# Six channel products moved into the attention steps, and kept products stored as upper and lower digits on two halves of the partitions

## The chip, the cores and the metric

One core of a Trainium2 chip runs the whole kernel. The time is the device time of one execution in microseconds (us); a profile is of one execution, taken by the hardware profiler, and its span is some 1.8 us shorter than that execution's own time. It can be of the slowest or of the fastest of a kernel's few executions, so spans are compared with care. Engines: PE is TensorE, PEld its weight loads, DVE is VectorE, ACT is ScalarE, POOL is GpSimd, SP is SyncE.

## The reference, cut to what matters

```python
x = attention(q, k, v, s)            # 8 batches x 576 tokens x 512 channels (8 heads x 64)
X = rfft(x, axis=1)                  # 64 modes are kept
Yr = Xr @ w_r - Xi @ w_i             # one 512x512 pair of weights for each mode
Yi = Xr @ w_i + Xi @ w_r
y = irfft(Y, n=576, axis=1)
u = x + y
return u + relu(u @ w_ch)            # w_ch: 512x512
```

The weights `w_r` and `w_i` are read once from memory, in 128 pieces, and most of the kernel's time passes while they arrive. The kernel uses `u @ w_ch = x @ w_ch + irfft(Y @ w_ch)`: the first term (the *product* of a pair of token tiles) needs no weight of the modes and can be made early and *kept*; the second, called v, is made chunk by chunk as the modes come.

## The kernel before

The work is cut into 18 pairs of 128-token tiles. Attention takes 32 steps; the modes of the fourth and last quarter of the channels then come in 8 chunks of 8 modes (0 to 7). Between these chunks the kernel makes the products of 16 pairs and keeps them in one of two ways. With way "e" the value is stored as two fp16 numbers, upper and lower digits, and TensorE puts it back (the *seed*: a product with the identity); with way "s" it is stored in fp32 and ScalarE puts it back.

```python
ways = dict(zip(kept, "esesessesesseses"))
def keep(i):
    x_times_wch(i, True)                      # 8 matmuls into zs[i], 128x1024 of PSUM
    ...
    if ways[i] == "e":                        # upper digits, then what is left
        nc.scalar.copy(out=z1s[i][:, 0], in_=zs[i])
        nc.vector.tensor_tensor(out=z1s[i][:, 1], in0=zs[i], in1=z1s[i][:, 0], op=ALU.subtract)
    else:
        nc.scalar.copy(out=z1s[i], in_=zs[i])
...
def seed(i):                                  # way "e": 4 matmuls of 128x512
    for x in range(2):
        for y in range(2):
            nc.tensor.matmul(zs[i][:, x, :], ident16h, z1s[i][:, y, x, :], start=(y == 0), ...)
...
TAKE = (3, 3, 1, 2, 4, 3)                     # works after chunks 0 to 5
for c in range(NCK - 2):
    yb = modes(NG - 1, c)
    for x in range(TAKE[c] - 1):
        work()                                # transposes one x, and makes the product of the one before
    yt = y_transposed(yb)
    work()
    y_times_wch(c, yt)                        # v of chunk c, then spread by a small DMA
...                                           # chunk 6, start_u(0), add_y of u
yb = modes(NG - 1, NCK - 1)                   # chunk 7: waits for the last weight
...                                           # its y and v
for i in range(NPRE):
    add_y(z_of(i), i, 1, slice(0, GK))        # v of chunks 0 to 6 into the first two pairs
```

`add_y` is the inverse transform of what has been spread. After chunk 7 the *tail* adds everything up for the 18 pairs and stores the result.

The softmax here doesn't subtract the row's maximum and nothing guards it: scores larger than these inputs give would overflow.

Of the kernel before, what the change touches and what calls it, by code (L numbers as in the profile page):

```python
# [9 lines left out]
FP32 = mybir.dt.float32  # L10
# [8 lines left out]
def kernel(  # L19
# [11 lines left out]
    nc = tc.nc  # L31
# [14 lines left out]
    MC = 8  # L46
    NCK = NM // MC
    WM = 4
    WB = 17
    LA = 3  # L50
    NF = NT - 1
    R = S // (P // 2)
# [23 lines left out]
    G_np[:, 1, :S] = -(cmv[:, None] * np.sin(ang.T))  # L76
    G_np = G_np.reshape(P, SP).astype(np.float16)

    d_ident16h = nc.inline_tensor(ident_np.astype(np.float16), name="c_ident16h").ap()
    d_ident32 = nc.inline_tensor(ident_np, name="c_ident32").ap()  # L80
    d_negm = nc.inline_tensor(
        np.concatenate([negm_np, negm4_np], axis=1).astype(np.float32), name="c_negm"
# [13 lines left out]
    y_acc = gp.tile([P, NCK, DM], FP32, name="y_acc")  # L96

    xs = [gp.tile([P, 5, 2, B, NM], BF16, name=f"xs{i}") for i in range(2)]
    ident16h = gp.tile([P, P], FP16, name="ident16h")
    Ff_sb = gp.tile([P, NT, 3 * NM], FP16, name="Ff_sb")  # L100
    G_sb = gp.tile([P, SP], FP16, name="G_sb")
    wch_sb = gp.tile([P, DT, DM], FP16, name="wch_sb")
    wpool = ctx.enter_context(tc.tile_pool(name="w_sb", bufs=WB))
    spool = ctx.enter_context(tc.tile_pool(name="small_sb", bufs=2))
    auxpool = ctx.enter_context(tc.tile_pool(name="aux_psum", bufs=2, space=PSUM))

# [78 lines left out]
    NE = len(early)  # L185
    wt = {}

    def loads_w(upto):
        todo = []
        while len(wt) < min(upto, len(wq)):  # L190
            g, c, ri, par = key = wq[len(wt)]
            if len(wt) < NE:
                t = early[len(wt)]
            else:
                t = wpool.tile([P, WM, DM], BF16, name="w_sb", tag="w")
            src = (moe_w_r, moe_w_i)[ri]
            todo.append((
                t,
                src[c * MC + par : (c + 1) * MC : 2, g * P : (g + 1) * P, :].rearrange("m p e -> p m e"),
            ))  # L200
            wt[key] = t
        return todo
# [14 lines left out]
    W0 = 3  # L217
    on_chip = []
    for n in range(N):
        w = W0 + (WB + NE - W0) * (n + 1) // (B + 1) if n < B else on_chip[-1] + 4  # L220
        on_chip.append(min(w, WB + (NE if used[n] < NE else used[n])))


    nc.sync.dma_start(out=s_sb, in_=s.rearrange("b h t -> (b h) t"))
# [3 lines left out]
    load(first[:2])  # L228
    load(loads_w(W0), first[2:] + tails0 + second)
    nc.sync.dma_start(out=Ff_sb, in_=d_Ff.rearrange("(T p) c -> p T c", p=P))  # L230
    nc.sync.dma_start(out=ident16h, in_=d_ident16h)
    nc.sync.dma_start(out=G_sb, in_=d_G)

    zero = ap_.tile([P, 16], FP32, name="zero")
# [60 lines left out]
    def transposes(n, which):  # L295
        if n >= N:
            return
        src = loaded[n][which]
        dA, dB = ((qtA, qtB), (ktA, ktB))[which]
        g, b = divmod(n, B)  # L300
        ps = trpool.tile([P, R, RP], BF16, name="tr_ps", tag="tr")
        for r in range(R):
            for h in range(2):
                rows = slice(D * h, D * h + D)
                nc.tensor.transpose(ps[rows, r, :], src[rows, r, :], ident16[rows, rows])  # L305
        for dst, rows in ((dA, slice(0, D)), (dB, slice(D, P))):
            copy = (nc.vector.tensor_copy, nc.scalar.copy)[which == 1 and dst is dB]
            copy(  # L308
                out=dst[n % NQ][rows, :].rearrange("d (p r) -> d p r", r=R),
                in_=ps[rows].rearrange("d r p -> d p r"),  # L310
            )
# [131 lines left out]
        nc.sync.dma_start(out=yv[16 * c : 16 * c + 16, :, which, :], in_=rows)  # L443


    with tc.tile_pool(name="sc_psum", bufs=2, space=PSUM) as scpool, \
            tc.tile_pool(name="tr_psum", bufs=1, space=PSUM) as trpool, \
            tc.tile_pool(name="av_psum", bufs=1, space=PSUM) as avpool:
        cum_rows(0)
        transposes(0, 0)  # L450
        transposes(0, 1)
        load(loads_qkv(2))
        pad_p()
        for n in range(N):
            if n in (0, 2):
                nc.vector.memset(xs[n // 2].rearrange("p k r b m -> p (k r b m)").bitcast(FP32), 0.0)
            tails_due = loads_tails(n // B + 1)[n % B - 3 : n % B - 2] if 2 < n % B < 5 else []
            load(loads_qkv(n + LA) + tails_due, loads_w(on_chip[n]))
            cum_rows(n + 1)
            scores(n, 0)  # L460
            av(n - 1, 1)
            transposes(n + 1, 0)
            scores(n, 1)
            transposes(n + 1, 1)
            fft(n - 1)
            av(n, 0)
            for c in mode_steps.get(n, []):
                modes(c // NCK, c % NCK)
            if n == N // 2:
                nc.gpsimd.dma_start(out=wch_sb, in_=moe_w_ch.rearrange("(dt p) e -> p dt e", p=P))  # L470
        av(N - 1, 1)
        fft(N - 1)
    load(loads_w(len(wq)))
    at.close()




    pairs = [((b, T), (b, T + 1)) for b in range(B) for T in range(0, NF, 2)]
    for i, b in ((4, 0), (10, B // 2)):  # L480
        pairs.insert(i, ((b, NF), (b + 2, NF)))
    NPRE = 2
    kept = list(range(NPRE, len(pairs)))


    ways = dict(zip(kept, "esesessesesseses"))

    finpool = ctx.enter_context(tc.tile_pool(name="fin_sb", bufs=1))
    yv = finpool.tile([P, B, 2, DM], FP16, name="yv")
# [11 lines left out]
    places = [finpool.tile([P, 4 * DM], BF16, name=f"z1_{i}") for i in range(NLOC)]  # L501
    places.append(old[:, 4 * DM : 8 * DM])
    places += [y_acc[:, c : c + 2, :].rearrange("p c e -> p (c e)").bitcast(BF16) for c in (0, 2)]
    xts, z1s, zs = {}, {}, {}

    def parts(b, T):

# [24 lines left out]

    def keep(i):
        x_times_wch(i, True)
        j = kept.index(i)
        if j < len(places):
            t = places[j]
        else:
            t = wpool.tile([P, WM, DM], BF16, name="z1", tag="w").rearrange("p m e -> p (m e)")
        if ways[i] == "e":  # L540
            z1s[i] = t.bitcast(FP16).rearrange("p (y x e) -> p y x e", y=2, x=2)
            nc.scalar.copy(out=z1s[i][:, 0], in_=zs[i])
            nc.vector.tensor_tensor(
                out=z1s[i][:, 1], in0=zs[i], in1=z1s[i][:, 0], op=ALU.subtract
            )
        else:
            z1s[i] = t.bitcast(FP32).rearrange("p (x e) -> p x e", x=2)
            nc.scalar.copy(out=z1s[i], in_=zs[i])  # L548

    def y_transposed(yb):  # L550
        ps = auxpool.tile([P, DT, P], FP16, name="yt_ps", tag="aux")
# [29 lines left out]
            i = ahead.pop(0)  # L581
            keep(i)

    order_z = list(kept)
    TAKE = (3, 3, 1, 2, 4, 3)
    us, rs = {}, {}
    GK = P - 2 * MC

# [64 lines left out]
    for c in range(NCK - 2):  # L653
        yb = modes(NG - 1, c)
        for x in range(TAKE[c] - 1):
            work()
        yt = y_transposed(yb)
        work()
        y_times_wch(c, yt)
    work()  # L660
    assert not order_z and not ahead
# [9 lines left out]

    start_u(0)
    add_y(us[0], 0, 0, slice(0, GK))
    yb = modes(NG - 1, NCK - 1)

    yt = spool.tile([P, DT, P], FP16, name="yt_sb", tag="yt")
# [14 lines left out]
        nc.vector.tensor_copy(out=vb[:, cols], in_=vp)  # L691
    spread(NCK - 1, 1, vb)
    for i in range(NPRE):
        add_y(z_of(i), i, 1, slice(0, GK))
    for i in range(NPRE):
        for cols in halves:
            add_last(z_of(i), i, vb, cols)
        relu(i, 2 - i)
# [5 lines left out]
    def seed(i):  # L704
        if ways.get(i) in ("e", "s"):
            zs[i] = zpool.tile([P, 2, DM], FP32, name="z_ps", tag="z")
        if ways.get(i) == "s":
            nc.scalar.copy(out=zs[i], in_=z1s[i])
        elif ways.get(i) == "e":
            for x in range(2):  # L710
                for y in range(2):
                    nc.tensor.matmul(  # L712
                        zs[i][:, x, :], ident16h, z1s[i][:, y, x, :],
                        start=(y == 0), stop=False, skip_group_check=True,
                    )

    def pre(i):
# [51 lines left out]
```

## Time and profile before

| | before |
|---|---|
| median of 4 runs beside the changed kernel | 461.33 us (460.58 to 462.08) |
| span in the profile, mean granted clock | 460.4 us, 0.873 |
| bytes read and written by transfers | 95.16 MB by the queues, 207 GB/s |
| the last weights' modes end | 422.06 us |
| first seed of the tail | 427.39 us |

The times are read from the timeline. Below is TensorE's timeline of before between 405 and 428 us; the columns are start, duration, engine and line, operation, tiles, sizes, the count, and in brackets the idle time before it with what ended it.

```profile
410.80 1.12 PE L419 MATMUL yp<-w_sb,xs 128*32 128x512 bf16 x16
412.72 0.40 PE L553 MATMUL yt_ps<-ident16h,y_sb 128*128 128x128 f16 x4 [0.26 <-DVE y_sb L433]
414.14 1.03 PE L561 MATMUL v_ps<-wch_sb,yt_sb 128*128 128x512 f16 x4
415.00 3.62 PE L528 MATMUL z_ps<-wch_sb,xs 128*128 128x512 f16 x16
421.61 0.45 PE L419 MATMUL yp<-w_sb,xs 128*32 128x512 bf16 x4 [1.29 <-DMA w_sb<-in_moe_w_i_dram]
```

The modes of chunk 6 (410.80) run as soon as the works are done. TensorE then waits 0.26 us for a y, and 1.29 us for the last weight at 421.61.

### The profile page before, as it was taken

How to read it: one execution, taken by the hardware profiler on the slowest of the kernel's cores; microseconds unless marked ns; L12 is line 12 of the kernel's file. 1: busy time of each engine (PE TensorE's matmuls, PEld its weight loads, DVE VectorE, ACT ScalarE, POOL GpSimd, SP SyncE). 2: the span in 40 equal slices, each digit the busy share in tenths (PEclk: the TensorE clock that was granted, in tenths of full speed). 3: DMA queues.
4: the chain of work that ended last, by engine and by line, in shares of the span. 5: the costliest groups of instructions: out<-in, count | busy, mean ns of one | idle time of the engine just before them, and what ended most of it. 6: DMA issues, size and time to landing. Idle time of an engine off the chain costs nothing.

```text
span 460.4 us, 10238 instructions
## 1 busy us (share of the span) xinstructions
PE 342.2 (74%) x4153; PEld 217.0 (47%) x4185; DVE 233.2 (51%) x521; ACT 218.4 (47%) x376; POOL 183.0 (40%) x269
## 2 busy tenths in 40 slices
PE   1779888974667668876666757567959858988995
PEld 1456666653445446654444534344635424544432
DVE  6775666663334346644334443334445625562675
ACT  1585876563444427744244342444602303340895
POOL 6754555544445455434544434444422222100000
PEclk9997999998777879978778795777878979999999
DMA  9999999999999999999999999999999999994697
GB/s 173 200 203 204 201 202 203 203 204 204 204 202 203 203 201 203 204 204 203 203 202 205 205 204 204 204 204 204 204 210 210 212 215 213 211 212 89 229 309 296
DMA packets 110063, 95.16 MB, mean 207 GB/s; under 512 B 28544, under 2 KB 105216, under 8 KB 110016
## 3 DMA queue, kind: packets, MB, share of 16 engines
q0 software_dynamic: 98960, 81.81, 112.2%
q1 hardware_dynamic: 11056, 12.70, 9.1%
q8 instruction: 33, 0.54, 0.4%
q14 instruction: 14, 0.11, 0.1%
HBM read 164.66 MB, written 9.44 MB: 378 GB/s over the span
## 4 chain that ended last, share of the span: by engine, by line
DMA 70%; PE 21%; issue 3%; DVE 3%; POOL 2%; SPq 0%; DVEq 0%; POOLq 0%
DMA w_sb<-in_moe_w_i_dram 31%; DMA w_sb<-in_moe_w_r_dram 25%; DMA q<-in_q_dram 7%; PE sc_ps L346 3%; PE sc_ps L340 2%; DMA wch_sb<-in_moe_w_ch_dram 2%; DMA v<-in_v_dram 2%; PE av_ps L375 2%; PE z_ps L593 2%; PE u_ps L612 2%; PE u_ps L593 2%; PE tr_ps L305 2%; PE yp L419 1%; PE z_ps L712 1%; PE z_ps L528 1%
## 5 line engine op out<-in xcount | busy, mean ns | idle before, releaser
L354 ACT ACTIVATE p_sb<-sc_ps,cumt_sb 128x576 f16<-128x576 f32 (+1 forms) x256 | 142.2, 635 | 57.2 <-PE sc_ps L346 57.0
L208 POOL DMA_DIRECT2D w_sb<-in_moe_w_i_dram x60 | 45.1, 753 | 74.8 <-PE yp L419 19.6
L208 POOL DMA_DIRECT2D w_sb<-in_moe_w_r_dram x60 | 45.2, 754 | 69.7 <-DMA w_sb<-in_moe_w_r_dram 33.2
L208 POOL DMA_DIRECT2D v<-in_v_dram x72 | 50.8, 707 | 36.0 <-DMA v<-in_v_dram 9.3
L305 PE MATMUL tr_ps<-ident,q 64*64 64x64 bf16 x576 | 18.8, 219 | 57.5 <-DMA q<-in_q_dram 57.5
L340 PE MATMUL sc_ps<-negm,ident 128*128 128x256 bf16 x256 | 58.2, 315 | 0.2
L419 PE MATMUL yp<-w_sb,xs 128*32 128x512 bf16 x480 | 37.0, 415 | 19.6 <-DMA w_sb<-in_moe_w_i_dram 18.7
L308 DVE COPY qtA<-tr_ps 64x576 bf16<-64x576 bf16 x32 | 23.8, 743 | 52.7 <-PE tr_ps L305 52.5
L325 ACT ACTIVATE p<-sc_ps,cumt 128x64 f16<-128x64 f32 x32 | 10.1, 314 | 84.1 <-PE sc_ps L321 84.1
L308 DVE COPY ktA<-tr_ps 64x576 bf16<-64x576 bf16 x32 | 24.0, 750 | 44.6 <-PE tr_ps L305 44.6
L375 PE MATMUL av_ps<-v,p_sb 128*128 128x65 f16 x1024 | 45.4, 199 | 0.0
L305 PEld LDWEIGHTS <-q 64*64 64x64 bf16 x576 | 14.8, 130 | 60.4 <-DMA q<-in_q_dram 59.5
L375 PEld LDWEIGHTS <-p_sb 128*128 128x128 f16 x1024 | 40.4, 101 | 5.2 <-issue 1.2
L346 PE MATMUL sc_ps<-qtB,ktB 128*128 128x64 bf16 (+2 forms) x160 | 37.6, 343 | 4.2 <-issue 3.1
L346 PE MATMUL sc_ps<-qtA,ktA 65*128 65x512 bf16 (+2 forms) x192 | 37.7, 306 | 0.5 <-DMA qtA<-ncum_sb 0.5
L528 PE MATMUL z_ps<-wch_sb,xs 128*128 128x512 f16 x144 | 37.0, 405 | 0.7 <-ACT z L548 0.7
L419 PEld LDWEIGHTS <-xs 128*32 128x32 bf16 x512 | 21.7, 172 | 29.6 <-issue 26.1
L380 DVE TENSOR_REDUCE den<-av_ps 128x5 f32<-128x10 f32 x64 | 10.8, 169 | 47.0 <-PE av_ps L375 46.9
L385 DVE TENSOR_TENSOR x_all<-av_ps,rcp 128x320 f16<-128x320 f32 x64 | 31.5, 492 | 2.2
L346 PEld LDWEIGHTS <-ktB 128*128 128x128 bf16 x192 | 23.9, 125 | 17.2 <-issue 8.8
L308 ACT COPY ktB<-tr_ps 64x576 bf16<-64x576 bf16 x32 | 20.3, 634 | 21.6 <-DVE ktA L308 21.1
L305 PE MATMUL tr_ps<-ident,k 64*64 64x64 bf16 x576 | 17.9, 213 | 15.0 <-DVE qtB L308 8.4
(96 smaller groups left out, 498.5 us busy)
## 6 DMA issues: line engine op xcount, KB each, us to landing
w_sb<-in_moe_w_r_dram POOLq DMA_DIRECT2D x60, 512.0 KB, 11.9
w_sb<-in_moe_w_i_dram POOLq DMA_DIRECT2D x60, 512.0 KB, 11.9
q<-in_q_dram POOLq DMA_DIRECT2D x32, 144.0 KB, 9.9
k<-in_k_dram POOLq DMA_DIRECT2D x32, 144.0 KB, 10.3
v<-in_v_dram POOLq DMA_DIRECT2D x72, 64.0 KB, 10.0
out_dram<-r_sb SPq DMA_DIRECT2D x16, 256.0 KB, 2.5
out_dram<-r_w SPq DMA_DIRECT2D x16, 256.0 KB, 2.6
x_all<-in_moe_w_i_dram POOLq DMA_DIRECT2D x3, 512.0 KB, 9.9
```

The costliest lines, as they stand in the source:

```text
L208: nc.gpsimd.dma_start(out=dst, in_=src)
L305: nc.tensor.transpose(ps[rows, r, :], src[rows, r, :], ident16[rows, rows])
L308: copy(out=dst[n % NQ][rows, :].rearrange("d (p r) -> d p r", r=R), in_=ps[rows].rearrange("d r p -> d p r"),)
L340: nc.tensor.matmul(ps[:, bass.ds(w * S, W)], ident16, negm[:, bass.ts(r, W)], start=True, stop=False, skip_group_check=True,)
L346: nc.tensor.matmul(ps[:, c0 : c0 + i1 - i0], keys[:, w, r, :], qt[:, i0:i1], start=False, stop=True, skip_group_check=True,)
L354: nc.scalar.activation(out=pt[:, poff[x] : poff[x] + S - w * W], in_=ps[:, w * S : (w + 1) * S - w * W], func=ACTF.Exp, bias=cumt_sb[:, x, ...
L375: nc.tensor.matmul(ps[:, I, r : r + NCH], lhsT, rhs, start=(i == 0), stop=(i == len(todo) - 1), skip_group_check=True,)
L380: nc.vector.tensor_reduce(out=den, in_=ps[:, :, 0 : VW : NCH], axis=mybir.AxisListType.X, op=ALU.add)
L385: nc.vector.tensor_tensor(out=x_all[:, g, b, :, D * h : D * h + D], in0=ps[:, :, 1 : NCH], in1=rcp.unsqueeze(2).to_broadcast([P, NT, D]), ...
L419: nc.tensor.matmul(ps[32 * cg : 32 * cg + 32, :], cols[:, c0 : c0 + 32, c * MC + 2 * cg + par], wt[(g, c, ri, par)][:, cg, :], start=(x == ...
L528: nc.tensor.matmul(z[:, x, :], xts[i][:, x, dt, :], wch_sb[:, dt, :], start=(dt == 0), stop=(last and dt == DT - 1), skip_group_check=True,)
L593: nc.tensor.matmul(dst[x][r, :], G_sb[rows, bass.ds(T * P, r.stop - r.start)], yv[rows, bb, which, :], start=start, stop=True, skip_group_ ...
```

## The change

The intent is to shorten the tail, the only part that doesn't wait for weights. Seeds of way "e" become cheaper on TensorE: the upper digits lie on one half of the partitions and the lower on the other, so one matmul of 64 columns with a "folding" identity adds them, and two such matmuls run beside each other on two column groups. Six products move into the last six attention steps. To find room for these six before attention's buffers are free, the ring of 17 weight buffers is divided into 11 and 6, and the 6 are given to kept products from weight 76 on. `TAKE` gets fewer works, and the `add_y` of the first two pairs goes ahead of the last modes.

```diff
-    WB = 17
+    WA, WB = 11, 6
...
-    ways = dict(zip(kept, "esesessesesseses"))
+    ways = dict(zip(kept, "eseseseseseseses"))
+    first_pairs = [i for i in kept if pairs[i][0][1] < NF and pairs[i][0][0] <= 3]   # six pairs
...
+        for y in range(2):                   # keep_product, way "e"
+            own, other = (slice((P // 2) * h, (P // 2) * (h + 1)) for h in (y, 1 - y))
+            nc.scalar.copy(out=z1s[i][own, y, xx], in_=z[own])
+            nc.vector.tensor_tensor(
+                out=z1s[i][other, y, xx], in0=z[own], in1=z1s[i][own, y, xx], op=ALU.subtract
+            )
...
+                first_transposed(i, 0)       # in attention step n, between its own work
...
-    TAKE = (3, 3, 1, 2, 4, 3)
+    TAKE = (2, 2, 1, 2, 0, 3)
...
+    for i in range(NPRE):
+        add_y(z_of(i), i, 1, slice(0, GK))
     yb = modes(NG - 1, NCK - 1)
...
-                        zs[i][:, x, :], ident16h, z1s[i][:, y, x, :],
-                        start=(y == 0), stop=False, skip_group_check=True,
+                        zs[i][(P // 2) * y : (P // 2) * (y + 1), x, :], fold16h, z1s[i][:, y, x, :],
+                        start=True, stop=False, skip_group_check=True,
+                        tile_position=(0, (P // 2) * y),
```

More of the change, by code (lines that the diff above doesn't have):

```diff
@@ L77 @@
     G_np = G_np.reshape(P, SP).astype(np.float16)
-    d_ident16h = nc.inline_tensor(ident_np.astype(np.float16), name="c_ident16h").ap()
+    ident16h_np = np.concatenate([ident_np, ident_np[:, : P // 2] + ident_np[:, P // 2 :]], axis=1)
+    d_ident16h = nc.inline_tensor(ident16h_np.astype(np.float16), name="c_ident16h").ap()
     d_ident32 = nc.inline_tensor(ident_np, name="c_ident32").ap()
@@ L98 @@
     xs = [gp.tile([P, 5, 2, B, NM], BF16, name=f"xs{i}") for i in range(2)]
-    ident16h = gp.tile([P, P], FP16, name="ident16h")
+    ident16h2 = gp.tile([P, P + P // 2], FP16, name="ident16h")
+    ident16h, fold16h = ident16h2[:, :P], ident16h2[:, P:]
     Ff_sb = gp.tile([P, NT, 3 * NM], FP16, name="Ff_sb")
@@ L102 @@
     wch_sb = gp.tile([P, DT, DM], FP16, name="wch_sb")
-    wpool = ctx.enter_context(tc.tile_pool(name="w_sb", bufs=WB))
+    wpool = ctx.enter_context(tc.tile_pool(name="w_sb", bufs=WA))
+    wpool2 = ctx.enter_context(tc.tile_pool(name="w2_sb", bufs=WB))
     spool = ctx.enter_context(tc.tile_pool(name="small_sb", bufs=2))
@@ L186, with ring_of @@
     wt = {}
+    LW2 = 76
+    def ring_of(k):
+        if k < NE:
+            return None
+        return int(k < LW2 and (k - NE) % (WA + WB) >= WA)
     def loads_w(upto):
@@ L191, in loads_w @@
             g, c, ri, par = key = wq[len(wt)]
-            if len(wt) < NE:
+            i = ring_of(len(wt))
+            if i is None:
                 t = early[len(wt)]
             else:
-                t = wpool.tile([P, WM, DM], BF16, name="w_sb", tag="w")
+                t = (wpool, wpool2)[i].tile([P, WM, DM], BF16, name="w_sb", tag="w")
             src = (moe_w_r, moe_w_i)[ri]
@@ L219 @@
     for n in range(N):
-        w = W0 + (WB + NE - W0) * (n + 1) // (B + 1) if n < B else on_chip[-1] + 4
-        on_chip.append(min(w, WB + (NE if used[n] < NE else used[n])))
+        w = W0 + (WA + WB + NE - W0) * (n + 1) // (B + 1) if n < B else on_chip[-1] + 5
+        nt, ring = 0, ([], [])
+        while nt < min(w, len(wq)):
+            i = ring_of(nt)
+            if i is not None:
+                depth = (WA, WB)[i]
+                if len(ring[i]) >= depth and ring[i][-depth] >= used[n]:
+                    break
+                ring[i].append(nt)
+            nt += 1
+        on_chip.append(nt)
     nc.sync.dma_start(out=s_sb, in_=s.rearrange("b h t -> (b h) t"))
@@ L230 @@
     nc.sync.dma_start(out=Ff_sb, in_=d_Ff.rearrange("(T p) c -> p T c", p=P))
-    nc.sync.dma_start(out=ident16h, in_=d_ident16h)
+    nc.sync.dma_start(out=ident16h2, in_=d_ident16h)
     nc.sync.dma_start(out=G_sb, in_=d_G)
@@ L443, in spread, with kept_place, keep_product, first_transposed @@
         nc.sync.dma_start(out=yv[16 * c : 16 * c + 16, :, which, :], in_=rows)
+    pairs = [((b, T), (b, T + 1)) for b in range(B) for T in range(0, NF, 2)]
+    for i, b in ((4, 0), (10, B // 2)):
+        pairs.insert(i, ((b, NF), (b + 2, NF)))
+    NPRE = 2
+    kept = list(range(NPRE, len(pairs)))
+    ways = dict(zip(kept, "eseseseseseseses"))
+    first_pairs = [i for i in kept if pairs[i][0][1] < NF and pairs[i][0][0] <= 3]
+    z1s, xts1 = {}, {}
+    def kept_place(i, t):
+        if ways[i] == "e":
+            z1s[i] = t.bitcast(FP16).rearrange("p (y x e) -> p y x e", y=2, x=2)
+        else:
+            z1s[i] = t.bitcast(FP32).rearrange("p (x e) -> p x e", x=2)
+    def keep_product(i, xx, z):
+        if ways[i] != "e":
+            nc.scalar.copy(out=z1s[i][:, xx], in_=z)
+            return
+        for y in range(2):
[4 more added lines that the diff above has]
+            )
+    def first_transposed(i, x):
+        b, T = pairs[i][x]
+        ps = auxpool.tile([P, DT, P], FP32, name="xt_ps", tag="aux")
+        for dt in range(DT):
+            nc.tensor.matmul(
+                ps[:, dt, :], x_all[:, dt, b, T, :], ident16h, start=True, stop=True,
+                skip_group_check=True,
+            )
+        xts1[i, x] = spool.tile([P, DT, P], FP16, name="xt1", tag="yt")
+        nc.vector.tensor_copy(out=xts1[i, x], in_=ps)
+    def first_product(i, x):
+        if x == 0:
+            t = wpool2.tile([P, WM, DM], BF16, name="z1", tag="w").rearrange("p m e -> p (m e)")
+            kept_place(i, t)
+        ps = auxpool.tile([P, DM], FP32, name="z1_ps", tag="aux")
+        for dt in range(DT):
+            nc.tensor.matmul(
+                ps, xts1[i, x][:, dt, :], wch_sb[:, dt, :], start=(dt == 0), stop=(dt == DT - 1)
+            )
+        keep_product(i, x, ps)
     with tc.tile_pool(name="sc_psum", bufs=2, space=PSUM) as scpool, \
@@ L463 @@
             scores(n, 1)
+            i = first_pairs[n - N + len(first_pairs)] if n >= N - len(first_pairs) else None
+            if i is not None:
+                first_transposed(i, 0)
             transposes(n + 1, 1)
@@ L466 @@
             av(n, 0)
+            if i is not None:
+                first_product(i, 0)
+                first_transposed(i, 1)
             for c in mode_steps.get(n, []):
                 modes(c // NCK, c % NCK)
+            if i is not None:
+                first_product(i, 1)
             if n == N // 2:
@@ L474 @@
     at.close()
-    pairs = [((b, T), (b, T + 1)) for b in range(B) for T in range(0, NF, 2)]
-    for i, b in ((4, 0), (10, B // 2)):
-        pairs.insert(i, ((b, NF), (b + 2, NF)))
-    NPRE = 2
-    kept = list(range(NPRE, len(pairs)))
-    ways = dict(zip(kept, "esesessesesseses"))
     finpool = ctx.enter_context(tc.tile_pool(name="fin_sb", bufs=1))
@@ L503 @@
     places += [y_acc[:, c : c + 2, :].rearrange("p c e -> p (c e)").bitcast(BF16) for c in (0, 2)]
-    xts, z1s, zs = {}, {}, {}
+    xts, zs = {}, {}
     def parts(b, T):
@@ L534, in keep @@
         x_times_wch(i, True)
-        j = kept.index(i)
+        j = late.index(i)
         if j < len(places):
@@ L539, in keep @@
             t = wpool.tile([P, WM, DM], BF16, name="z1", tag="w").rearrange("p m e -> p (m e)")
-        if ways[i] == "e":
-            z1s[i] = t.bitcast(FP16).rearrange("p (y x e) -> p y x e", y=2, x=2)
-            nc.scalar.copy(out=z1s[i][:, 0], in_=zs[i])
-            nc.vector.tensor_tensor(
-                out=z1s[i][:, 1], in0=zs[i], in1=z1s[i][:, 0], op=ALU.subtract
-            )
-        else:
-            z1s[i] = t.bitcast(FP32).rearrange("p (x e) -> p x e", x=2)
-            nc.scalar.copy(out=z1s[i], in_=zs[i])
+        kept_place(i, t)
+        keep_product(i, slice(0, 2), zs[i])
     def y_transposed(yb):
@@ L582, in work @@
             keep(i)
-    order_z = list(kept)
-    TAKE = (3, 3, 1, 2, 4, 3)
+    late = [i for i in kept if i not in first_pairs]
+    order_z = list(late)
+    TAKE = (2, 2, 1, 2, 0, 3)
     us, rs = {}, {}
@@ L657 @@
         yt = y_transposed(yb)
-        work()
+        if TAKE[c]:
+            work()
         y_times_wch(c, yt)
@@ L693 @@
     for i in range(NPRE):
-        add_y(z_of(i), i, 1, slice(0, GK))
-    for i in range(NPRE):
         for cols in halves:
```

## The prediction

> **What bounds the kernel now.** I read the page's slices first, then the chain that ended last, then the timeline of the last 60 us, then the waits of the attention steps.
>
> ```profile
> PE   1779888974667668876666757567959858988995
> DMA  9999999999999999999999999999999999994697
> GB/s 173 200 203 204 201 202 203 203 204 204 204 202 203 203 201 203 204 204 203 203 202 205 205 204 204 204 204 204 204 210 210 212 215 213 211 212 89 229 309 296
> ```
>
> A slice is 11.5 us. For 36 slices the DMA row stands at 9 and the rate at 200 to 215 GB/s, while PE is often at 6 or 7: up to about 418 us the weight stream (w_r, w_i) sets the pace. Then PE is at 8 and 9: the last 40 us are TensorE's. The chain says the same:
>
> ```profile
> DMA 70%; PE 21%; issue 3%; DVE 3%; POOL 2%; SPq 0%; DVEq 0%; POOLq 0%
> ```
> ```profile
> 398.48 23.09 DMA w_sb<-in_moe_w_i_dram
> 421.61 0.48 PE yp L419 x3
> ```
>
> The last weight, issued at 398.48, lands at 421.6; the last mode chunk (c = 7) can only then be ended. The tail is 460.4 - 421.6 = 38.8 us. From 427.39 (first seed) to 455.4 TensorE has 16 pairs of 6 matmuls (0.215 us each, 1.29 us a pair), 7 seeds of 4 matmuls (0.86 us) and 0.7 us more for the two pairs of 64-row tiles: 20.6 + 6.0 + 0.7 = 27.4 of 28.0 us. So the tail is bound by TensorE.
>
> During attention a step takes some 12.4 us, and TensorE waits in it for q:
>
> ```profile
> 298.00 0.69 PE L305 MATMUL tr_ps<-ident,q 64*64 64x64 bf16 x18 [5.22 <-DMA q<-in_q_dram]
> 310.40 0.69 PE L305 MATMUL tr_ps<-ident,q 64*64 64x64 bf16 x18 [3.92 <-DMA q<-in_q_dram]
> 322.91 0.69 PE L305 MATMUL tr_ps<-ident,q 64*64 64x64 bf16 x18 [3.52 <-DMA q<-in_q_dram]
> ```
>
> Without the wait a step is about 12.4 - 3.9 = 8.5 us: there is room of 3.5 to 5.2 us for other work.
>
> **What the Trainium skill says.** (1) "TensorE: Matmul & The Clock Gate", section "Measured speedup vs the span model": three column tiles of 32 run 2.38 times as fast as one after the other. The trace agrees in kind. Sixteen matmuls of modes on four column groups take 1.05 us start to start, not 16 x 0.215. For two groups of 64 columns, which is what the new seed uses:
>
> ```profile
> 441.92 0.62 PE L593 MATMUL z_ps<-yv,G_sb 128*64 128x512 f16 x4
> 442.47 0.62 PE L612 MATMUL u_ps<-x_all,ident16h 64*64 64x512 f16 x4
> 443.02 0.62 PE L593 MATMUL u_ps<-yv,G_sb 128*64 128x512 f16 x4
> 443.58 1.04 PE L712 MATMUL z_ps<-z,ident16h 128*128 128x512 f16 x4
> ```
>
> Four of them take 0.55 us from start to start, against 0.86 for four whole ones: 1.56 times, not 2. (2) "TensorEngine Tiling (Array Packing)", "PSUM Bottleneck": tiling speeds up TensorE, not the evacuation. In the tail ScalarE has a relu or a seed of 1.02 us nearly back to back, so the gain has a floor there. (3) "VectorE: DVE Perf Modes", the errata section: its table counts free elements, not partitions. By it 1024 elements out of PSUM cost (172 + 1024)/1.2 GHz = 1.00 us on ScalarE and (120 + 1024)/0.96 GHz = 1.19 us on VectorE; the trace has 1.01 and 1.22. So a copy over half the partitions costs as much as over all. (4) "DMA: Bandwidth & Descriptors", "Queues, rings and completion order": an engine goes round robin between the queue rows that have work. In the trace the small y and v spreads take 5.5 to 6.2 us while weights stream, and 2.9 us at 422.9, when they don't.
>
> **The change part by part.**
>
> *(a) Seeds on column groups.* Before, 7 "e" pairs: 7 x 0.86 = 6.0 us of TensorE in the tail. After, 8 (one "s" becomes "e"): 8 x 0.55 = 4.4 us. Saved 1.6 us; ScalarE loses a 1.02 us seed copy as well. Two pairs (one e, one s) then take 0.55 + 2 x 1.29 = 3.13 us on TensorE; ScalarE has two relus and one seed, 3.05 us. That is so close that I take 1.5.
>
> *(b) add_y of the first two pairs ahead of the last modes.* Four matmuls of 0.215 us, at 424.35 in the trace, leave the tail: 0.86 us. But they filled the wait for the second half of the v cast, so I take 0.7. In their new place they wait for the v spread of chunk 6, which before was issued at 415.92 and landed 5.5 us later, at 421.4, just ahead of the last weight. If it is no later, the four stand beside it for nothing; if it is later, TensorE stands in front of the last modes.
>
> *(c) Six pairs in attention.* The final stage loses 6 of 16 works (x transposed 0.44, product 1.73 us: 13 us of TensorE), but that stage waits for weights, so this gives nothing by itself. What it gives is room for the rest.
>
> *(d) Kept products on two halves.* An "e" product was one ScalarE copy and one VectorE subtract of 128x1024:
>
> ```profile
> 402.65 1.01 ACT L542 CAST z<-z_ps 128x1024 f16<-128x1024 f32 x1 [3.17 <-PE z_ps L528]
> 403.69 1.23 DVE L543 TENSOR_TENSOR z<-z_ps,z 128x1024 f16<-128x1024 f32 x1 [1.42 <-ACT z L542]
> ```
>
> 2.25 us in a row. Now it is two of each over 64 partitions, at the same cost each, and in the built program the second ScalarE copy waits for the first VectorE subtract: four in a row, 4.5 us. After chunk 5 four works follow (e, s, e, s), as many as before. I walked them by hand from the end of modes 5, with 1.01, 1.22, 0.62 (x casts), 0.26 and 1.73 us. VectorE takes its queue in program order, so the x casts of the second next work stand behind the subtracts. Modes 5 would end at 398.5 rather than 400.3 (no work before it now; its last weight landed at 397.9). The first e is free at 405.5, the second product starts at 407.0, modes 6 at 411.4 (before 410.8). But the second subtract of pair 16 holds VectorE to 413.5, then come v of chunk 5 and y of chunk 6: y is ready at 414.9 (before 412.7), v of chunk 6 at 418.2 (before 415.9). Landed with some 4 us: 422.2. Then four add_y and all modes 7, ending at about 424.2, against 422.05. Cost: 2.1 us at worst of my walk.
>
> *(e) Ring of 11 in place of 17 from weight 76.* By the formula for weights on chip, 103 of 128 are asked for at the end of attention (before 109). The stream need not stop for that: attention ends with fewer weights before it. But blocks 29, 30 and 31 of four weights each may only be issued after modes of the step before. A step with an "s" pair becomes 8.5 + two transposes 0.6 + two products 2.0 + wait for the PSUM buffer 0.7 = 11.8 us; with an "e" pair the chain of four adds 2 us: 13.7. Four weights take 4 x 0.524 MB / 213 GB/s = 9.85 us. The surplus is 3.3, 1.3 and 1.0 us in the last three steps (the last has no transposes); some 3 us of queue stand against it. Idle stream: 2.6 us, if my steps are right.
>
> **The sum.** Tail: -1.5 - 0.7 = -2.2 us. Against it 2.1 (d) and 2.6 (e), both from walks that add waits one after the other where the hardware may have slack, and the author evidently re-tuned the order of works; I count 40% of each: +1.9 us. 461.0 - 2.2 + 1.9 = 460.7 us.
>
> **Rivals.** *First: only the tail counts.* Neither the ring nor the longer chain reaches the stream: last weight at 421.5, v of chunk 6 before it. For it: TensorE idles 3.5 to 5.2 us a step, and POOL waits for queue room rather than for slots in most gaps. Then 461.0 - 2.2 = 458.8, and with seeds at the full factor of two (0.43) one more us less: 457.8. *Second: the stream is starved* by the ring of 11 in the last attention steps and the last weight lands 3 to 6 us later. For it: before the change TensorE already waited for single weights at 268.97 and 281.94, so the ring was never far ahead. Then 462 to 466. *Third: v of chunk 6 takes the weight's place* as what the last modes wait for: 460 to 461.5. *Fourth: ScalarE binds the tail* at 3.05 us per two pairs: (a) is then worth 1.2, not 1.6.
>
> **Range and chances.** The cheapest combination is 457.8 and the dearest 461.0 - 1.9 + 2.1 + 5 = 466.2. A range of 457.0 to 465.5 covers most of it. Two per cent is 9.2 us: 451.8 is under everything that the tail can give, and 470.2 needs a starved stream for 7 us and more. Faster 0.01, within 0.96, slower 0.03.
>
> **What would show it.** In the changed profile: (a) the seed's four matmuls start to start at 0.55 us (0.43 would make it 1 us better, 0.86 refute it); (b) the z add_y before the last modes, waiting for the v spread or not; (d) copies and subtracts of 64x1024 alternating at 1.0 and 1.2 us, and the y of chunk 6 ready at about 415; (e) the GB/s row dipping under 195 around 310 to 350 us, and the last weight landing after 422.5. If the row doesn't dip, the second rival falls. Wrong I would be if the last weight landed well before 420 or after 427, since the bytes to be moved are the same.

## More of the kernel before

At 415.00 the sixteen matmuls of two products take 3.62 us, 0.22 us each.

```profile
377.77 3.32 PE L528 MATMUL z_ps<-wch_sb,xs 128*128 128x512 f16 x8
```

These are eight matmuls, and the granted clock of the window from 372 to 378 us is 0.65.

## The result, and the profile after

| | before | after |
|---|---|---|
| median (4 runs each) | 461.33 us | 468.44 us (468.13 to 468.96) |
| ratio | | 1.0153, 95% 1.0136 to 1.0170 |
| span in the profile | 460.4 us | 467.2 us |
| the last weights' modes end | 422.06 us | 430.00 us |
| from there to the end (the tail) | 38.3 us | 37.2 us |

A ratio is taken over the runs of both kernels in the same rounds, so it isn't quite the ratio of the medians quoted. The kernel became 1.5% slower: within 2%, as expected, but outside the predicted range. The tail gained 1.1 us. Everything before it lost 7.9 us. The slices of the page of after, to be held against those in the prediction:

```profile
PE   1779878955663888768396687697868685679995
DMA  9999999999999999999999999999999999991698
GB/s 173 200 203 203 201 202 203 204 204 204 204 204 197 202 201 204 204 204 204 196 202 204 204 204 205 203 204 203 203 199 210 209 210 215 211 177 35 217 301 315
```

PE is busier at the end of attention, where the six products now are. The DMA row stays at 9 through that stretch, and the rate dips to 199 GB/s only once there. In the 36th slice it falls to 177 and in the 37th to 35, where before there were 212 and 89 (a slice is 11.7 us here and was 11.5): the weights had *arrived*, and the core moved hardly anything while TensorE was not yet ready for the last of them. So the stream hardly ended later (from 300 to 422 us 24.82 MB were moved, before 24.85); its end is no longer what the last modes wait for. The shares of the chain that ended last agree: DMA goes from 70 to 55%, and "issue" from 3 to 12%.

```profile
DMA 55%; PE 22%; issue 12%; DVE 5%; POOL 5%; ACT 1%; DVEq 0%; POOLq 0%
```

The same chain in order of time (start, duration, what) shows what took the weights' place:

```profile
401.18 2.95 PE z_ps L603 x8
404.15 1.01 ACT y_acc L496
405.19 1.23 DVE y_acc L497
406.44 1.02 ACT y_acc L496
407.48 1.24 DVE y_acc L497
408.74 1.30 DVE xs L597 x2
410.48 3.41 PE z_ps L603 x8
413.92 1.01 ACT z L496
414.95 1.23 DVE z L497
416.20 1.02 ACT z L496
417.24 1.24 DVE z L497
```

It is copy, subtract, copy, subtract, 4.5 us in a row, twice (y_acc and z are the two places in which these products are kept). After the first four come two casts of x on VectorE, whose queue they stood in behind the subtracts, and only then the next product. TensorE's timeline of after, from the end of chunk 5 to chunk 7:

```profile
400.98 3.14 PE L603 MATMUL z_ps<-wch_sb,xs 128*128 128x512 f16 x8
...
409.48 0.38 PE L593 MATMUL xt_ps<-ident16h,x_all 128*128 128x128 f16 x4 [2.97 <-DVE xs L597]
...
410.30 3.58 PE L603 MATMUL z_ps<-wch_sb,xs 128*128 128x512 f16 x8
...
414.58 1.89 PE L603 MATMUL z_ps<-wch_sb,xs 128*128 128x512 f16 x8
416.40 1.12 PE L441 MATMUL yp<-w_sb,xs 128*32 128x512 bf16 x16
...
419.97 0.40 PE L621 MATMUL yt_ps<-ident16h,y_sb 128*128 128x128 f16 x4 [1.90 <-DVE y_sb L455]
...
421.54 1.91 PE L629 MATMUL v_ps<-wch_sb,yt_sb 128*128 128x512 f16 x4
423.25 3.98 PE L603 MATMUL z_ps<-wch_sb,xs 128*128 128x512 f16 x16
...
428.88 1.12 PE L441 MATMUL yp<-w_sb,xs 128*32 128x512 bf16 x16
```

Two things are to be seen. TensorE waits 2.97 us for a cast and 1.90 us for the y of chunk 6. And the work *after* each wait is slow: the product at 410.30 takes 3.58 us for eight matmuls where the one at 414.58 takes 1.89; the v at 421.54 takes 1.91 where before had 1.03. The windows of 6 us say why (busy time and counts by engine, then the granted TensorE clock, the DMA share and the rate); first before, then after:

```profile
408.00:414.00 6.00, 5.33 (x48) 2.77 (x46) 3.85 (x6) 2.62 (x3) 0.00 (x0) 1.00 1.24 206
420.00:426.00 6.00, 4.13 (x38) 2.43 (x31) 1.61 (x4) 0.80 (x3) 0.00 (x0) 1.00 0.11 28
```
```profile
408.00:414.00 6.00, 4.30 (x18) 1.86 (x18) 3.19 (x5) 1.06 (x3) 0.00 (x0) 0.72 1.24 207
420.00:426.00 6.00, 5.79 (x28) 2.86 (x29) 3.09 (x5) 0.59 (x1) 0.00 (x0) 0.72 0.26 65
```

The clock was 1.00 in both windows before, and is 0.72 in both after: for part of each window TensorE ran at half speed. The prediction's walk had no such term, although the trace of before shows one (377.77 above).

### The profile page after: what moved, and what is told of

The parts are those of the page before. It is cut to its first block, busy times and chain, and to the rows that moved or that the text cites. A ratio compares the mean times of both kernels' runs of the same rounds, so it can differ in the third digit from the quotient of the medians.

```text
span 467.2 us, 10261 instructions
## 1 busy us (share of the span) xinstructions
PE 344.6 (74%) x4157; PEld 214.4 (46%) x4189; DVE 245.9 (53%) x536; ACT 227.0 (49%) x392; POOL 182.7 (39%) x269
## 4 chain that ended last, share of the span: by engine, by line
DMA 55%; PE 22%; issue 12%; DVE 5%; POOL 5%; ACT 1%; DVEq 0%; POOLq 0%
DMA w_sb<-in_moe_w_i_dram 28%; DMA q<-in_q_dram 10%; DMA w_sb<-in_moe_w_r_dram 5%; DMA v<-in_v_dram 3%; POOL w_sb L220 3%; PE av_ps L397 3%; PE sc_ps L368 2%; DMA x_all<-in_moe_w_r_dram 2%; PE z_ps L603 2%; DMA k<-in_k_dram 2%; PE tr_ps L327 2%; PE yp L441 2%; PE sc_ps L362 2%; PE z_ps L662 2%; DMA y_acc<-in_moe_w_r_dram 2%
## 5 line engine op out<-in xcount | busy, mean ns | idle before, releaser
L362 PE MATMUL sc_ps<-negm,ident 128*128 128x256 bf16 x256 | 56.9, 309 | 1.3 <-ACT p_sb L376 1.0
L327 PE MATMUL tr_ps<-ident,q 64*64 64x64 bf16 x576 | 17.8, 213 | 49.1 <-DMA q<-in_q_dram 49.1
L441 PE MATMUL yp<-w_sb,xs 128*32 128x512 bf16 x480 | 38.3, 436 | 17.0 <-DMA w_sb<-in_moe_w_i_dram 8.1
L368 PE MATMUL sc_ps<-qtB,ktB 128*128 128x64 bf16 (+2 forms) x160 | 34.7, 321 | 3.5 <-issue 2.2
L368 PEld LDWEIGHTS <-ktB 128*128 128x128 bf16 x192 | 22.4, 117 | 14.8 <-issue 6.1
L496 ACT CAST z<-z_ps 64x512 f16<-64x512 f32 (+1 forms) x18 | 13.0, 722 | 33.1 <-PE z_ps L518 14.7
L327 PE MATMUL tr_ps<-ident,k 64*64 64x64 bf16 x576 | 16.9, 206 | 15.9 <-DVE qtB L330 10.0
```

The source lines that it names most:

```text
L327: nc.tensor.transpose(ps[rows, r, :], src[rows, r, :], ident16[rows, rows])
L362: nc.tensor.matmul(ps[:, bass.ds(w * S, W)], ident16, negm[:, bass.ts(r, W)], start=True, stop=False, skip_group_check=True,)
L368: nc.tensor.matmul(ps[:, c0 : c0 + i1 - i0], keys[:, w, r, :], qt[:, i0:i1], start=False, stop=True, skip_group_check=True,)
L441: nc.tensor.matmul(ps[32 * cg : 32 * cg + 32, :], cols[:, c0 : c0 + 32, c * MC + 2 * cg + par], wt[(g, c, ri, par)][:, cg, :], start=(x == ...
L496: nc.scalar.copy(out=z1s[i][own, y, xx], in_=z[own])
```

## The experiments

The theory after reading the traces (*chain*): the doubled chain of copies and subtracts holds TensorE between chunks 5 and 7, waits and cold products together. The rivals: the *ring* of 11 buffers holds up the weights; the *add_y* in its new place holds up the last modes. Thirteen kernels ran, all correct; the kernel before ran beside each (461.5 to 461.9 us). Runs 1 to 4 shared a chip and the runs of the kernel before, so did 5 to 8, 9 to 11, and 12 and 13.

### 1. Two works moved away from the last chunks

```diff
-    TAKE = (2, 2, 1, 2, 0, 3)
+    TAKE = (2, 2, 1, 2, 2, 1)
```

> The changed kernel with TAKE (2, 2, 1, 2, 2, 1) in place of (2, 2, 1, 2, 0, 3): two of the four works that follow the modes of chunk 5 are done after chunk 4 instead. Chain theory (the copies and subtracts of an e product, four in a row of 1.0 and 1.2 us, hold up TensorE and VectorE between chunks 5 and 7): two works fewer there, modes of chunk 6 start near 410 instead of 416.4, those of chunk 7 end near 423.5 instead of 429.9: 462 us (461 to 463.5). Ring theory (the ring of 11 slots makes the weight stream end later) and add_y theory (the moved add_y waits in front of the last modes): no gain, 467 to 469.

Measured: 464.73 us, ratio 1.0050 (1.0017 to 1.0083). More than half of the loss is gone, so the chain's place after chunk 5 matters. But the expected 462 was missed, and TensorE's timeline shows what was left:

```profile
421.74 1.46 PE L662 MATMUL z_ps<-yv,G_sb 112*128 112x512 f16 x4 [1.98 <-issue]
423.13 1.96 PE L441 MATMUL yp<-w_sb,xs 128*32 128x512 bf16 x16
```

Now that TensorE was early, the moved `add_y` waited 1.98 us, for the spread of v of chunk 6 (the page names only "issue"; the four matmuls read that tile), and the last modes behind it ran at 1.96 instead of 1.12 us. This is the prediction's third rival, hidden in the changed kernel by the larger delay.

### 2. Kept products whole again

```diff
-        for y in range(2): ...   # copy and subtract of each half
+        nc.scalar.copy(out=z1s[i][:, 0, xx], in_=z)
+        nc.vector.tensor_tensor(out=z1s[i][:, 1, xx], in0=z, in1=z1s[i][:, 0, xx], op=ALU.subtract)
```

with the old seeds of four whole matmuls. 

> The changed kernel with e products kept as before (one copy and one subtract over 128 partitions, seeds of four whole matmuls); six early pairs, rings, TAKE and the moved add_y stay. Chain theory: two links of 2.25 us in a row instead of four, modes of chunk 7 some 4.4 us earlier, the tail 1.3 us longer (the tail of the changed kernel was 1.1 us shorter than before): 465.3 us (464 to 466.5). Ring and add_y theories: only the tail changes, 469.5 us.

Measured: 463.51 us, ratio 1.0035 (1.0009 to 1.0061); the last modes began at 421.95 instead of 428.88 us, and the clock was 1.00 in all windows from 408 to 426 us. Undoing this one part brings back 4.9 of the 7.1 us by the medians, even though the cheaper seeds go with it. That is better than the expected range. Of the 1.2 us of span that are left against before, 1.0 lies ahead of the tail: the last modes, which here too stand behind the moved `add_y`, end at 423.07 us against 422.06.

### 3. The ring alone, on the kernel before

```diff
-    WB = 17
+    WA, WB = 11, 6            # and the pacing of the changed kernel
```

> The kernel before with the two rings (11 and 6 slots, from weight 76 on 11 alone) and the new pace of loads, nothing else: no early pairs, no split, no moved add_y. Ring theory: most of the loss is here, 466 us or more. Chain theory: TensorE is no busier in attention, so slots come free in time: 461 to 463 us.

Measured: 461.55 us, ratio 0.9993 (0.9970 to 1.0016). The ring by itself costs nothing. The ring as cause falls.

### 4. The split alone, on the kernel before

The copies and subtracts by halves and the column-group seeds, nothing else. 

> The kernel before with e products kept on two halves and seeded by column groups, nothing else: ring of 17, all 16 products in the last stage, seven of them e. Chain theory: four e products among the eight works after chunks 4 and 5 each take 2.25 us longer, so the end is later than in the changed kernel although the seeds save 7 x 0.31 us: 469 us (466 to 474). Ring theory: the chain is hidden behind the weights and only the seeds count: 459 to 460 us.

Measured: 471.32 us, ratio 1.0198 (1.0175 to 1.0222). TensorE's timeline repeats the pattern of the changed kernel, twice within 14 us:

```profile
398.94 0.38 PE L520 MATMUL xt_ps<-ident16h,x_all 128*128 128x128 f16 x4 [2.97 <-DVE xs L524]
...
399.76 2.97 PE L530 MATMUL z_ps<-wch_sb,xs 128*128 128x512 f16 x8
...
412.90 0.38 PE L520 MATMUL xt_ps<-ident16h,x_all 128*128 128x128 f16 x4 [2.97 <-DVE xs L524]
...
413.72 3.27 PE L530 MATMUL z_ps<-wch_sb,xs 128*128 128x512 f16 x8
```

With 3 in place, runs 2 and 4 settle which part costs: the split of the kept products. Without the other parts of the change the split is dearer still, by some 3 us (471.32 against 468.44); which of these parts helps is not shown.

### 5. The add_y alone put back

```diff
-    for i in range(NPRE):                      # ahead of the last modes
-        add_y(z_of(i), i, 1, slice(0, GK))
     yb = modes(NG - 1, NCK - 1)
...
+    for i in range(NPRE):                      # after v of chunk 7, as before
+        add_y(z_of(i), i, 1, slice(0, GK))
```

> The changed kernel with the add_y of the first two pairs back behind the last v, nothing else. add_y theory (it holds the last modes back): 2 us or more faster, 466 us or less. Chain theory: in the changed kernel TensorE reached these add_y without a wait (427.93, right after the one before), so they only change places: 468.3 us (467.5 to 469).

Measured: 468.36 us, ratio 1.0143 (1.0125 to 1.0160), as expected: in the changed kernel the move is neutral.

### 6. Both: works moved, add_y put back

The edits of 1 and 5 together. 

> Both: TAKE (2, 2, 1, 2, 2, 1) and the add_y back. In the run with the new TAKE alone TensorE did wait there: 1.98 us for the v of chunk 6, issued at 416.15, landed near 421.7, and then ran its modes at half the clock. With the add_y back the last modes wait only for the last weight (about 421.6): 464.7 - 2.5 to 4 = 461 us (460 to 462.3), so the kernel before or up to 1 us better. If the add_y do not matter: 464.5 us.

Measured: 461.64 us (6 runs), ratio 1.0013 (0.9996 to 1.0029). The loss is gone. The last modes again wait for the last weight:

```profile
421.87 0.45 PE L441 MATMUL yp<-w_sb,xs 128*32 128x512 bf16 x4 [1.62 <-DMA w_sb<-in_moe_w_i_dram]
```

So the `add_y`, neutral in the changed kernel, cost something once the other delay was removed. How much is less sure: 3.1 us by the medians (464.73 against 461.64, on different chips), 1.7 us by the ratios, whose intervals just overlap; in the traces the last modes end at 422.32 us here and at 425.09 in run 1. The costs don't add up: each hides behind the other. That this version doesn't beat the kernel before was as expected, though its profiled span (459.4 us, of one execution) was 1 us shorter.

### 7 and 8. All six early products of way "e"

The idea: if only two "e" pairs are left for the last chunks, the doubled chain goes into attention, where TensorE waits for q anyway. In 7 the pairs were permuted so; 8 adds the edits of 6.

```diff
+    es = firsts + [others[1], others[3]]
+    ss = [p for p in others if p not in es]
+    pairs = pairs[:NPRE] + [p for es_ss in zip(es, ss) for p in es_ss]
...
+    late.sort(key=lambda i: ways[i] == "s")
```

> The changed kernel with the pairs in another order: the six early products are all e, so only two e products are left for the last stage and they go first; the four works after chunk 5 are all s. TAKE and add_y as in the changed kernel. Chain theory: modes of chunk 6 start near 410 although four works still stand there, and the end is at 462.5 us (461 to 464.5), about what the whole keep gave less 1 us for the seeds. Rival (the number of works after chunk 5, not the kind of keep): 468 us. Rival (six e chains in attention now hold up the weights): 468 us or more, with the last weight later than 421.6.

> All three: only two late e products, TAKE (2, 2, 1, 2, 2, 1), add_y back. Chain theory: like the run with TAKE and add_y back or up to 1 us better, 460.5 us (459.5 to 462), the tail 1.1 us shorter than before and the rest as before. Rival (early e chains hold up the weights): 464 us or more.

Measured: 467.75 us, ratio 1.0129 (1.0110 to 1.0149), and 467.61 us, ratio 1.0133 (1.0118 to 1.0147). Both missed. What happened in run 8 is in its row of rates:

```profile
GB/s 172 200 203 203 201 202 203 203 204 204 204 204 200 203 202 203 204 204 204 197 201 204 204 204 205 203 202 201 183 153 166 210 215 212 214 213 126 188 339 296
```

In the slices from 29 to 31 (some 325 to 360 us) the stream falls to 153 GB/s (in run 7 to 151). The longest waits of POOL for the modes that free a weight buffer were 10.67 and 9.38 us, against 9.0 in the changed kernel and 2.4 before in the same stretch; the last weight landed at 427.68 instead of 421.6. An early product is kept in two pieces of 512 columns, so its chain is twice 0.58, 0.68, 0.58 and 0.69 us, and the modes of the step stand behind the first of the two:

```profile
352.12 1.12 PE L441 MATMUL yp<-w_sb,xs 128*32 128x512 bf16 x16 [2.51 <-DVE z L503]
```

Here the prediction's second rival is real: twelve chains of some 2.6 us in the attention steps hold up the modes, the buffers come free late, and the weights stop. That the ring of 11 has a part in it is argued, not shown: no run has these products with the ring of 17. The changed kernel, with three of the six early products of way "s", loses far less (see (e) below).

Run 7 shows two things more (its profile is of its fastest execution, 465.60 us). From the last weight of chunk 5 to the modes of chunk 6 it needed 11.67 us (402.75 to 414.42), the changed kernel 16.85 (399.55 to 416.40): four works stand there in both, but no "e" in run 7, so it is the kind of keep that counts, as the chain theory said. And the moved `add_y` waited again, ahead of the last modes:

```profile
425.02 1.02 PE L669 MATMUL z_ps<-yv,G_sb 112*128 112x512 f16 x4 [1.93 <-issue]
```

### 9. The casts of x ahead of the subtracts

The copies and subtracts of a product are put into the queues one work later, so that VectorE casts the next x first. 

> The changed kernel with the copies and subtracts of a kept product issued one work later, behind the x casts of the next work (same instructions, another order in the queues of ScalarE and VectorE). If what delays TensorE after chunk 5 is that the x casts stand behind the two subtracts in VectorE's queue: modes of chunk 6 start 2 to 3 us earlier than 416.4, 465.5 us (464.5 to 466.5). If it is that the chain of four holds its PSUM buffer too long, order does not matter: 468 us.

Measured: 467.25 us, ratio 1.0121 (1.0097 to 1.0144). Nearer to the order theory's rival than to its own 465.5: 1.2 us less than the changed kernel by the medians, but the intervals of the two ratios overlap, so a gain from the order is not shown. Chunk 6 came 2.5 us earlier (413.89; 0.5 of it because the last weight of chunk 5 did), but the wait only moved:

```profile
409.48 1.89 PE L603 MATMUL z_ps<-wch_sb,xs 128*128 128x512 f16 x8 [2.02 <-DVE y_acc L497]
```

The third product needs the PSUM buffer of the first, which is held until its last subtract. Two buffers and a chain of 4.5 us leave TensorE waiting whichever comes first.

### 10 and 11. Two of the late "e" pairs added by VectorE instead

Way "v" keeps fp32 and lets VectorE add it in the tail, with no chain and no seed. Run 10 is run 6 with two late pairs so, run 11 the kernel before with two.

```diff
-    ways = dict(zip(kept, "eseseseseseseses"))
+    ways = dict(zip(kept, "esesesesesvsesvs"))
```

> TAKE (2, 2, 1, 2, 2, 1), add_y back, and two of the late e pairs kept whole in fp32 and added by VectorE in the tail (way v, which the kernel has and does not use): two chains of 4.5 us fewer in the last stage, two seeds of 0.55 us fewer on TensorE and two relus fewer on ScalarE in the tail, 2.8 us more on VectorE, which has 6 us to spare there. Tail 1.1 us shorter than in the run with TAKE and add_y back (461.6): 460.5 us (459.5 to 461.5).

> The kernel before with two of its seven e pairs made v pairs, nothing else. Control for the run with two v pairs: two seeds of 0.86 us fewer in a tail bound by TensorE: 461.7 - 1.7 = 460 us (459.5 to 461.5). If this is as fast as the other or faster, what is gained there is the v pairs' and not the change's.

Measured: 462.02 us, ratio 0.9999 (0.9979 to 1.0019), and 463.39 us, ratio 1.0044 (1.0019 to 1.0069). Both missed: no gain, and in run 11 a loss. In the tail of run 11 TensorE had one wait of 1.74 us for a seed of ScalarE, where before had none.

### 12. The waits filled with useless products

This asks whether the half clock after the waits counts, apart from the waits. The products of pairs 15 and 17 are issued twice; the second time only puts the same value into the same place. The chain of copies stays.

```diff
+    TWICE = (15, 17)
...
-        for x in range(2):
+        for x in list(range(2)) * (2 if i in TWICE else 1):
```

> The changed kernel, with the products of pairs 15 and 17 issued a second time: 16 useless matmuls that put the same value into the same buffer again, and lie in the two waits of TensorE (some 406 to 409 and 417 to 420 us) in which nothing else is ready. Theory, that these waits cost twice, once as waits and once through the half clock that follows them (the products after them took 3.58 instead of 1.89 us): the clock row stays at full in 408 to 426 us and the last modes end about 3 us earlier; 465.4 us (464.5 to 466.5), although TensorE does more. Rival, that only the waits themselves count and the clock is incidental: the same or slower, 468.4 to 470 us.

Measured: 465.80 us (465.28 to 466.30), ratio 1.0089 (1.0061 to 1.0117). TensorE does sixteen matmuls *more*, and the kernel is 2.6 us faster than the changed one by the medians; the intervals of the ratios are apart. The profiled spans differ by 3.7 us, but they are of the slowest execution of the one and the fastest of the other. The windows of run 12:

```profile
408.00:414.00 6.00, 4.97 (x29) 2.50 (x29) 3.74 (x6) 2.04 (x4) 0.00 (x0) 1.00 1.24 206
414.00:420.00 6.00, 5.34 (x50) 2.91 (x49) 4.98 (x7) 2.46 (x3) 0.00 (x0) 1.00 0.94 162
420.00:426.00 6.00, 6.00 (x41) 2.85 (x39) 0.71 (x2) 0.00 (x0) 0.00 (x0) 1.00 0.14 32
```

The clock is full in all three, where the changed kernel had 0.72, 1.00 and 0.72. The product after the first wait now takes 1.89 us:

```profile
409.63 1.89 PE L605 MATMUL z_ps<-wch_sb,xs 128*128 128x512 f16 x8
```

From the start of the modes of chunk 6 (415.77) to those of chunk 7 (425.24) it is 9.47 us; in the changed kernel 428.88 - 416.40 = 12.48. Of the 3.64 us by which the last modes come earlier, 3.0 lie there. What was slow in the changed kernel adds up to the same: 1.69 (410.30) + 0.88 (421.54) + 0.36 (423.25) = 2.9 us. The first of these gains passes through the y of chunk 6, which VectorE can only make after the second chain. Chunk 6 itself is only 0.6 us earlier, since the useless product of pair 17, 1.73 us, stands ahead of it; the last weight of chunk 5 had landed earlier by as much in this execution (398.82 against 399.55 us).

### 13. The same for the wait for the last weight in run 6

The product of pair 1 issued twice. 

> The version with earlier copies of x and with add_y back in its old place (461.6 us), with the product of pair 1 issued a second time to fill TensorE's wait for the last weight. If the tail suffers from a clock that drops in that wait: 460.8 us (460 to 461.6). If the tail's clock is not touched by that wait: 461.6 us (461.2 to 462), as without it.

Measured: 462.25 us, ratio 1.0006 (0.9985 to 1.0027): no gain. In run 6 the clock was already 1.00 from 420 to 432 us and 0.99 after, so there was nothing to win by keeping TensorE warm there.

No version that ran beats the kernel before.

## Why the prediction was wrong

The number (460.7, range 457.0 to 465.5) was wrong by 7.7 us; the class, within 2%, was right. By its steps:

- **(a) Seeds on column groups: right.** From their start to that of the next work it was 0.46 to 0.56 us where nothing else was waited for. TensorE was busy 26.43 us from first seed to last pair against 28.01, so 1.58 us were saved, as worked out. But the tail now begins its first `add_y` before the spread of the last v has landed, and waits 0.45 us for it; and the stretch after the last pair was 0.3 us longer.
- **(b) add_y moved: mis-sized.** It gave about 0.3 us between the last modes and the first seed, not 0.7: the four matmuls had been filling a wait for the v cast. With (a) this makes the tail's 1.1 us instead of 2.2. The doubt that TensorE would stand in front of the last modes was right in kind and hidden here; run 1 shows it.
- **(c) Six early products give nothing by themselves:** not tested alone; run 4 doesn't tell them from the other parts.
- **(d) The chain of four: the mechanism was right, the size was not, and this is the step that failed.** The walk had the last modes end at 424.2 us, 2.1 later than before; they ended at 430.0, 7.9 later. The difference is 5.8 us. Most of it is a term that the walk lacked: it took every product at full speed, and four groups ran in part at half: 1.25 (400.98: 3.14 for 1.89), 1.69, 0.88 and 0.36 us, together 4.2. The rest belongs to (e): the walk let chunk 5 end at 398.5, and it ended at 400.2, since its last weight landed 1.6 us later than before: 1.7 us. The two make 5.9. Run 12 shows 3.0 of the 4.2 by taking them away; the 1.25 us at 400.98, after a wait for weights, were not tested, and stayed in run 12; run 2 had a slow product there too (3.62 us at 399.92) and lost little by it.
- **Counting 40% of (d) and (e) was wrong too.** The discount stood for slack that the walk might have missed. A walk that follows one engine's queue in program order can just as well miss a cost, and here it did. But even with both in full, 461.0 - 2.2 + 4.7 = 463.5 us would have been 4.9 us short.
- **(e) The stream set back: right in kind, smaller, and not by the ring alone.** From 300 to 398 us the transfers moved 20.53 MB before, as much in run 3 (the ring alone), 20.52 in run 2 (the ring and the early products, kept whole), and 20.19 in after: 0.34 MB less, 1.6 us at the 211 GB/s of before, where the prediction had 2.6. These are single profiles; the runs with the same early products on two halves had 20.14 to 20.43. So it took the doubled chains in the attention steps, and the lost bytes account for the late last weight of chunk 5. (The prediction's surpluses of 3.3, 1.3 and 1.0 us don't follow from its own steps, either: 13.7 and 11.8 less 9.85 are 3.9 and 2.0.) By the last weight most of it was made up: run 6, with the same early products, got it at 421.87 us, before at 421.61. These are the waits of POOL in after between 300 and 420 us (total us, times, longest), where before had 14.9 us in 8 waits, the longest 2.4:

```profile
POOL w_sb L220 <- PE yp L441: 48.1, 8, 9.0
```

  The small loss of bytes says that the queue had enough in it to cover most of them. With twice as many chains, in runs 7 and 8, it had not.
- **The rivals.** The first (only the tail counts) fell. The second (stream starved) gave the nearest range, 462 to 466, but not for its reason: the last modes didn't wait for the last weight, and the ring by itself cost nothing (run 3). The third was real behind the delay of (d) (runs 1 and 7). The fourth didn't bind: ScalarE was busy 23.98 of the 26.88 us from first seed to last pair.

What stays open: the 1.25 us at 400.98, and how much of (e) is the ring's. The 4.5 us in a row come from the built program, in which the second copy waits for the first subtract. Putting both copies first doesn't take that away: in a build of that form the first subtract waits for both copies, which is four in a row again; it wasn't run.

## What to carry to other kernels

Cutting an evacuation of PSUM into halves of the partitions halves no duration (64x1024 took 1.01 and 1.22 us, 128x1024 1.01 and 1.23): count each piece at full price, and count them in a row where two engines take turns on one bank. In a stretch where TensorE is nearly the bound, price a new wait of some 2 to 3 us at more than its length, because the work behind it may run at half clock (here 2.97 us brought 1.69 more, and 1.90 us 1.24), and look at the clock in windows of a few us before trusting a hand walk. And undo suspects in pairs, not only one by one: the `add_y` looked free until the larger delay in front of it was gone.

## What the Trainium skill lacked or had wrong

- "TensorE: Matmul & The Clock Gate", section "HAM oscillation — how this bites in real kernels", gives the rule as no gaps of TensorE over about 3.4 us. Here shorter ones were followed by half speed: after 2.97 us eight matmuls took 3.58 instead of 1.89 us, and after 1.90 us (with 0.20 more a moment later) four took 1.91 instead of 1.03. It isn't a matter of one gap's length alone: in run 9 a gap of 2.02 us was followed by a product at full speed, in run 1 one of 1.98 us by half speed. The page does tell, in its section "A second HAM failure mode: psum-queue depth-cycling", of a kernel whose clock swung with frequent short idles, but with no lengths. Its advice to keep TensorE busy (section "Why this matters for your kernels") was borne out: useless matmuls in the gaps made the kernel 2.6 us faster (run 12).
- The same page, section "Measured speedup vs the span model", has 4 row tiles, 3 column tiles and grids, but no measured figure for two column groups of 64. Here four such matmuls of 512 columns took 0.55 us from start to start against 0.86 whole: 1.56 times.
- "PSUM — Partial Sum Buffer", section "Terms", says that different quadrants of one bank may be accessed at the same time. In the program built here a ScalarE copy of one half of the partitions waited for VectorE's subtract of the other half of the same banks: 1.0, 1.2, 1.0, 1.2 us in a row. No run here shows whether the chip would allow both at once; the page doesn't say that a built program may order them all the same.
